# Loading x and the experts' matrices of a soft mixture of experts in rows of 2 KB

## The chip, the core and the metric

The kernel runs on one core of a Trainium2 chip. The metric is the device time of one launch in microseconds (us). The kernel before took 889.4 us as the median of three runs (888.58, 889.4 and 891.3).

## What is computed

Two stages stand behind one another. The first is a long causal convolution per channel of u = x * v with a filter that a small network computes from position features; its result is multiplied by x again. The reference uses Fourier transforms, the kernel matrix products. The second is a soft mixture of experts over all 45,824 tokens of 128 features that the first stage gives:

```python
logits = x @ phi                                  # (N, 32): 8 experts, 4 slots each
d = exp(logits - logits.max(0)); d /= d.sum(0)    # over the tokens, per slot
slot_input = d.T @ x                              # (32, 128): dispatch
for e in range(8):
    slot_out[e] = maximum(slot_input[e] @ w1[e], 0) @ w2[e]   # w1: 128x1024, w2: 1024x128
c = exp(logits - logits.max(1)); c /= c.sum(1)    # over the slots, per token
out = c @ slot_out                                # (N, 128): combine
```

All data are float32.

## The kernel before

The convolution runs over eight groups of channels. Its last phase (`p4`, seven steps of the list ORDER, lines 623 to 636) multiplies by x (`p4_gate`, or `p4_gate_apart` on GpSimd) and stores the result to a scratch buffer in HBM, `scr`, features as rows and tokens as columns (`p4_out`, line 465; `p4_rest`, line 471). The tokens stand there in pieces, two for each step of ORDER: most of 3,296 tokens, one of 2,884 and two last ones of 44 and 48. A row of a piece is one contiguous run.

The second stage (`Moe` and `_moe`) reads `scr` back in 23 blocks of 2,048 tokens (NB = 16 times 128; the last has 768). A block is a tile of 128 partitions (features) by 2,048 tokens, 1 MB, with rows of 8 KB. `Moe.load` (line 692) issues one DMA for each piece that a block touches, so one or two a block (line 700). Where the buffers are:

- blocks 0 to 4 go to `ahead_buf`, in the place where the experts' matrices will be. Their first 112 rows (d0 = 0 to D - CG) are loaded while the convolution's last group is still on its way (`weights`, line 655), the last 16 rows (d0 = 112) in `ahead` (line 722) when these have been stored. Blocks 5 to 9 (`xbuf`) follow in `ahead` too, between the stores of the last steps.
- the loop of `_moe` works on pairs of blocks. Blocks i and up are transposed (`turn`, line 714), and `fetch(i)` (line 952) then issues what comes into the buffer that is free now: for i below 10 the block i + 10, for 10 to 13 two experts' `w1` each (`load_w1`, line 670, 512 KB with rows of 4 KB), for 14 the `w2` of experts 0 to 2 (`load_w2`, line 673, the same size), for 15 to 17 the blocks 20 to 22, then the other `w2`.
- step m of the loop has, on TensorE in this order: the transposes of block 2m, the logits (line 780) of blocks 2m + 2 and 2m + 3, the transposes of block 2m + 1, the dispatch sums of pair m - 1 (line 872) and the running maximum (line 820). The last pair but one that is whole, blocks 20 and 21, has its logits in step 9.

After the last block the dispatch sums become the slots' inputs, the experts run (lines 1067 to 1106), and the combine step (`spread`, line 1120) makes one output tile after another (line 1128) and stores it in 1 MB DMAs (line 1136).

Every load and store of this part is issued by SyncE, one behind the other. Instructions inside `inorder(...)` keep the program's order; the loads of x and of the matrices are not in it, and their place is a scheduler's. A DMA is issued when the buffer that it overwrites has been read, when what it reads has landed, and when the semaphore that it will use is free of its last transfer.

Of the kernel before, what the change touches and what calls it, by code (L numbers as in the profile page):

```python
# [17 lines left out]
B, S, D = 4, 11456, 128  # L18
# [27 lines left out]
FF = 1024  # L46
# [592 lines left out]
class Moe:  # L639
# [3 lines left out]
    XB = 5  # L643
    OB = 4
    CB = 8 * NB

    def __init__(self, tc, cp, scr, phi, mw1, mw2, rep, out):
        self.tc, self.cp, self.scr, self.out = tc, cp, scr, out
        self.phi, self.mw1, self.mw2, self.rep = phi, mw1, mw2, rep

        self.blocks = [(q, min(self.NB, QN - q)) for q in range(0, QN, self.NB)]
        self.xt, self.xq = {}, {}
        self.pieces = sorted(_pieces().values())
# [14 lines left out]
            self.load(i, 0, D - CG)  # L668

    def load_w1(self, e):  # L670
        self.tc.nc.sync.dma_start(out=self.w1t[:, e], in_=self.mw1[e])

    def load_w2(self, e):
        self.tc.nc.sync.dma_start(out=self.w2t[e],
                                  in_=self.mw2[e])

    def logit_banks(self):
        self.pls = self.ctx.enter_context(ExitStack())
# [3 lines left out]
    def places(self):  # L682
# [4 lines left out]
        bufs = [self.xreg[:, i * sz : (i + 1) * sz] for i in range(n)]  # L687
        far = [self.E[:, self.CB * NSLOT + i * sz :][:, :sz] for i in range(2)]
        self.xbuf = bufs[: self.XB - 1] + far[:1]
        self.obuf = bufs[self.XB - 1 :] + far[1:]  # L690

    def load(self, i, d0=0, d1=D):
        q0, n = self.blocks[i]
        t = (self.ahead_buf if i // self.XB in (0, 2) else self.xbuf)[i % self.XB][:, : 128 * n]
        z0, z1 = 128 * q0, 128 * (q0 + n)
        for a, m in self.pieces:
            lo, hi = max(z0, a), min(z1, a + B * m)
            if lo < hi:
                src = self.scr[D * a : D * (a + B * m)].rearrange("(d t) -> d t", d=D)
                self.tc.nc.sync.dma_start(out=t[d0:d1, lo - z0 : hi - z0], in_=src[d0:d1, lo - a : hi - a])  # L700
        self.xt[i] = t.rearrange("p (q t) -> p q t", t=128)

    def turn(self, pool, tag, i, k0, k1, shared=False):
# [28 lines left out]
def _moe(mo):  # L732
# [11 lines left out]
    ereg = mo.E  # L744
    far = mo.CB * NSLOT + 4 * FF
    Cms = [ereg[:, : mo.CB * NSLOT], ereg[:, far : far + (QN - mo.CB) * NSLOT]]
    Cms = [c.rearrange("p (q s) -> p q s", s=NSLOT) for c in Cms]
    csum = ereg[:, QN * NSLOT + 4 * FF :][:, :QN]

    def weights_of(q0, n):  # L750
        assert (q0 < mo.CB) == (q0 + n <= mo.CB)
        return Cms[0][:, q0 : q0 + n] if q0 < mo.CB else Cms[1][:, q0 - mo.CB : q0 - mo.CB + n]

# [198 lines left out]
    def fetch(i):  # L952
        if i < 2 * XB:
            mo.load(i + 2 * XB)
        elif i < 2 * XB + 4:
            for e in range(2 * (i - 2 * XB), 2 * (i - 2 * XB) + 2):
                mo.load_w1(e)
        elif i < 3 * XB:
            for e in range(3):
                mo.load_w2(e)  # L960
        elif i + XB < NBL:
            mo.load(i + XB)
        else:
            for e in range(3 + 2 * (i + XB - NBL), min(NEXP, 5 + 2 * (i + XB - NBL))):
                load_w2(e, i)
# [330 lines left out]
```

## Time and profile before

| | |
|---|---|
| median of three runs | 889.4 us |
| profiled execution | 892.43 us |
| its span, from the first to the last instruction | 890.7 us |
| TensorE busy with matmuls | 857.9 us (96%) |
| VectorE, ScalarE, GpSimd busy | 80%, 51%, 44% |
| DMA over the span | 197.02 MB, 221 GB/s on the mean, 94,386 packets |
| granted TensorE clock, mean | 0.992 |

A busy share is a mean over unlike stages. A DMA share of 1.0 means that all 16 DMA engines are occupied by packets; it says nothing of how fast these are, for which the rate in GB/s stands beside it. "Issue" in the chain of waits is time in which an engine waited for nothing that the profile shows.

### The profile page before, as it was taken

The numbers are of one execution on the slowest core, as the hardware profiler recorded it, in microseconds if no ns is written. First come the engines' busy times: TensorE is split into PE (matmuls) and PEld (weight loads), VectorE is DVE, ScalarE is ACT, GpSimd is POOL, SyncE is SP. The second block draws the span as 40 slices with busy tenths as digits, with TensorE's granted clock in tenths as the row PEclk, the third lists the DMA queues.
The fourth block names the chain that finished last, engine by engine and source line by source line (L and its number), as shares of the span: only waits on it lengthen the run. The fifth ranks groups of instructions, "written<-read, shape, count | busy, mean of one in ns | idle before, by whom it ended". The sixth has DMA issues, their size and how long they took to land. (4 is left out here: it accounts for less than half of the span.)

```text
span 890.7 us, 37282 instructions
## 1 busy us (share of the span) xinstructions
PE 857.9 (96%) x16192; PEld 791.0 (89%) x16192; DVE 714.5 (80%) x1239; ACT 455.1 (51%) x971; POOL 393.1 (44%) x538
## 2 busy tenths in 40 slices
PE   9999999999999999999999999999999999899991
PEld 8998989999999999999999999999999987566540
DVE  5967976799799889988988998899789058786791
ACT  5775558315811851472166128415811637887761
POOL 5003860492088019405910960393078013775750
PEclk9999999999999999999999999999999999999996
DMA  9963684457747754775486376557716979993698
GB/s 323 396 197 117 204 246 153 144 155 254 207 135 207 234 166 128 237 237 172 132 261 202 120 222 214 168 166 247 218 44 173 272 176 374 412 355 121 277 416 365
DMA packets 94386, 197.02 MB, mean 221 GB/s; under 512 B 14329, under 2 KB 55707, under 8 KB 90382
## 3 DMA queue, kind: packets, MB, share of 16 engines
q1 hardware_dynamic: 94046, 194.50, 67.0%
q8 instruction: 128, 2.10, 0.9%
q14 instruction: 36, 0.29, 0.1%
q10 hardware_dynamic: 144, 0.07, 0.0%
q0 software_dynamic: 32, 0.07, 0.0%
HBM read 137.73 MB, written 56.86 MB: 218 GB/s over the span
## 5 line engine op out<-in xcount | busy, mean ns | idle before, releaser
L350 POOL TENSOR_TENSOR T<-m 111x256 f32<-111x256 f32 (+1 forms) x199 | 150.9, 758 | 344.8 <-DVE m L344 344.8
L344 DVE TENSOR_TENSOR m<-p,T 111x1024 f32<-111x1024 f32 (+1 forms) x175 | 200.4, 1205 | 14.4 <-PE p L340 7.6
L360 PE MATMUL p<-tab,T 111*99 111x112 f32 x2048 | 205.4, 260 | 1.4 <-POOL T L351 0.3
L360 PEld LDWEIGHTS p<-tab,T 111*99 111x99 f32 x2048 | 198.8, 170 | 6.5 <-issue 1.6
L340 PE MATMUL p<-T,W 128*64 128x128 f32 (+1 forms) x3168 | 197.3, 276 | 0.4 <-issue 0.3
L425 ACT ACTIVATE vc<-p 128x412 f32<-128x412 f32 (+1 forms) x112 | 51.7, 513 | 266.4 <-PE p L412 227.0
L340 PEld LDWEIGHTS p<-T,W 128*64 128x64 f32 (+1 forms) x3168 | 182.0, 127 | 2.8 <-DVE m L344 0.6
L412 PE MATMUL p<-tab,E 99*64 99x103 f32 (+1 forms) x3584 | 174.0, 252 | 1.6 <-DVE E L373 0.6
L412 PEld LDWEIGHTS p<-tab,E 99*64 99x64 f32 x3584 | 166.2, 136 | 3.8 <-ACT vc L425 0.8
L375 ACT ACTIVATE E<-p 99x448 f32<-99x448 f32 x254 | 131.9, 575 | 63.9 <-PE p L360 57.8
L351 POOL TENSOR_TENSOR T<-m 111x256 f32<-111x256 f32 (+1 forms) x199 | 147.4, 741 | 0.0
L186 ACT ACTIVATE T<-p 128x396 f32<-128x396 f32 x240 | 100.2, 535 | 11.3 <-PE p L174 11.1
L174 PE MATMUL p<-tab1x,x 53*64 53x99 f32 x3648 | 86.7, 246 | 0.2 <-ACT E L224 0.2
L174 PEld LDWEIGHTS p<-tab1x,x 53*64 53x64 f32 x3648 | 79.8, 132 | 4.4 <-ACT E L224 0.4
L443 DVE TENSOR_TENSOR p<-p,vc 128x824 f32<-128x824 f32 (+1 forms) x46 | 47.0, 1022 | 8.9 <-ACT vc L425 8.9
L268 DVE TENSOR_TENSOR x<-x,T 128x448 f32<-128x448 f32 x51 | 31.6, 619 | 21.2 <-DMA x<-in_xf_dram 11.6
L274 DVE TENSOR_TENSOR x<-T 128x224 f32<-128x224 f32 x102 | 39.2, 426 | 1.8
L270 DVE TENSOR_TENSOR T<-x 128x224 f32<-128x224 f32 x102 | 39.2, 426 | 1.7
L224 ACT ACTIVATE E<-fl 111x512 f32<-111x512 f32 (+1 forms) x50 | 26.8, 627 | 21.3 <-PE fl L218 21.3
L451 DVE TENSOR_TENSOR E<-p,E 128x824 f32<-128x824 f32 x36 | 36.6, 1017 | 1.2
L720 ACT ACTIVATE xreg<-pt 128x512 f32<-128x512 f32 (+1 forms) x68 | 35.0, 609 | 1.0 <-PE pt L714 0.9
L344 DVE TENSOR_TENSOR m<-p,E 111x1024 f32<-111x1024 f32 (+1 forms) x25 | 28.7, 1201 | 5.1 <-PE p L340 4.9
(156 smaller groups left out, 972.1 us busy)
## 6 DMA issues: line engine op xcount, KB each, us to landing
x<-in_xf_dram SPq DMA_DIRECT2D x114, 256.0 KB, 4.2
out_dram<-xreg SPq DMA_DIRECT2D x16, 1024.0 KB, 10.6
E<-in_xi_dram SPq DMA_DIRECT2D x37, 412.0 KB, 3.9
T<-in_vf_dram SPq DMA_DIRECT2D x65, 224.0 KB, 5.1
scr<-E SPq DMA_DIRECT2D x67, 206.0 KB, 4.3
T<-hs SPq DMA_DIRECT2D x63, 154.0 KB, 4.5
hs<-E SPq DMA_DIRECT2D x12, 784.0 KB, 4.6
mv<-in_vf_dram SPq DMA_DIRECT2D x42, 224.0 KB, 4.6
```

The costliest lines, as they stand in the source:

```text
L174: inorder(nc.tensor.matmul(ps[h][RP * d : RP * d + RP, i, s, :], lhsT=sd[js, i, s, d, :], rhs=tab1x[js, J * (s + d) : J * (s + d + 1)], st ...
L186: inorder(nc.scalar.activation(dst, src, AF.Copy))
L270: inorder(eng.tensor_tensor(out=vt[:, :, m : m + 2], in0=xr[:, :, 0:2], in1=xr[:, :, 2:4], op=op))
L340: inorder(nc.tensor.matmul(ps[ns, i].rearrange("p b c -> p (b c)"), lhsT=W[:, k0 + i, ns], rhs=Tf[:, :, k0 + i, :], start=True, stop=True, ...
L344: inorder(nc.vector.tensor_mul(m[:, :n].rearrange("p k s e c i -> p k s (e c i)").rearrange("p k s (b c) -> p k s b c", c=CG), ps[:, :n].u ...
L350: inorder(eng.tensor_tensor(out=Ty[:, 0], in0=m[:, :n, 0, 0], in1=m[:, :n, 1, 1], op=ALU.subtract))
L351: inorder(eng.tensor_tensor(out=Ty[:, 1], in0=m[:, :n, 1, 0], in1=m[:, :n, 0, 1], op=ALU.add))
L360: inorder(nc.tensor.matmul(pk[:, i, 2 * s : 2 * s + 2, :].rearrange("p q r -> p (q r)"), lhsT=T[0:N1, s, 2 * k + i, u // 2, :, u % 2], rhs ...
L375: inorder(nc.scalar.activation(dst, src, AF.Copy))
L412: inorder(nc.tensor.matmul(pv[RP * h : RP * h + RP, 2 * k + i, w, j0:], lhsT=E[:J, r, 2 - 2 * w + s, :], rhs=tab4[:, s, o + j0 : o + NJ], ...
L425: inorder(nc.scalar.activation(vc[:, w, :, j0:], pv[:, :, 0, j0:], AF.Copy, scale=2.0 * w - 1.0))
L443: inorder(nc.vector.tensor_tensor(out=pw[:, :, :, j0:], in1=vc[:, :, :, j0:], op=ALU.add, in0=pw[:, 1:2, :, j0:].to_broadcast([128, 2, 4, ...
```

## The change

`Moe` gets a constant RUN = 512. `load` cuts what it reads of a piece at every 512 tokens of the block, where the first row is 0 (`d0 == 0`), so that a transfer has rows of 2 KB at most; with d0 = 112, the last 16 rows of blocks 0 to 4, it stays as it was. `load_w1` and `load_w2` load an expert's matrix in two halves with rows of 2 KB.

```diff
+    RUN = 512
 
     def load_w1(self, e):
-        self.tc.nc.sync.dma_start(out=self.w1t[:, e], in_=self.mw1[e])
+        for f in range(0, FF, self.RUN):
+            self.tc.nc.sync.dma_start(out=self.w1t[:, e, f : f + self.RUN], in_=self.mw1[e, :, f : f + self.RUN])
 
     def load_w2(self, e):
-        self.tc.nc.sync.dma_start(out=self.w2t[e],
-                                  in_=self.mw2[e])
+        n = self.RUN // 128
+        for j in range(0, FF // 128, n):
+            self.tc.nc.sync.dma_start(out=self.w2t[e][:, j : j + n], in_=self.mw2[e, :, j : j + n])
 
         for a, m in self.pieces:
-            lo, hi = max(z0, a), min(z1, a + B * m)
-            if lo < hi:
-                src = self.scr[D * a : D * (a + B * m)].rearrange("(d t) -> d t", d=D)
+            lo, end = max(z0, a), min(z1, a + B * m)
+            src = self.scr[D * a : D * (a + B * m)].rearrange("(d t) -> d t", d=D)
+            while lo < end:
+                hi = min(end, z0 + ((lo - z0) // self.RUN + 1) * self.RUN) if d0 == 0 else end
                 self.tc.nc.sync.dma_start(out=t[d0:d1, lo - z0 : hi - z0], in_=src[d0:d1, lo - a : hi - a])
+                lo = hi
```

## Rows read from the trace of the kernel before

**Rows 1.** Windows: stretch, length, busy us by engine, clock, DMA share, GB/s.

```profile
840.00:860.00 20.00, 19.28 (x116) 8.50 (x112) 18.87 (x34) 14.75 (x27) 18.20 (x29) 1.00 1.01 417
```

**Rows 2.** Chain of waits, 640 us to the end: start, length, what.

```profile
771.66 0.95 issue
...
778.60 0.70 issue
...
784.97 1.03 issue
...
801.80 1.92 PE pl L780 x16
...
814.13 0.62 issue
...
828.99 3.07 PE pw L1128 x23
```

**Rows 3.** The page, DMA queues: packets, MB, share of 16 engines.

```profile
q8 instruction: 128, 2.10, 0.9%
```

**Rows 4.** TensorE's waits, 757 to 829: total us, times, longest.

```profile
PE pt L714 <- issue: 1.6, 2, 1.0
```

**Rows 5.** Windows again, columns as in the first group.

```profile
12.00:15.00 3.00, 3.00 (x30) 3.00 (x29) 2.08 (x4) 1.19 (x2) 0.40 (x2) 1.00 1.05 354
15.00:18.00 3.00, 3.00 (x29) 2.85 (x28) 2.54 (x5) 1.64 (x5) 0.00 (x0) 1.00 1.05 382
18.00:21.00 3.00, 2.83 (x24) 2.46 (x26) 2.94 (x11) 0.85 (x3) 0.00 (x0) 1.00 1.05 387
...
757.00:775.00 18.00, 15.67 (x322) 9.90 (x317) 14.47 (x25) 16.90 (x37) 13.54 (x14) 1.00 1.02 415
775.00:790.00 15.00, 13.27 (x298) 9.22 (x294) 11.23 (x23) 11.94 (x27) 11.09 (x14) 1.00 1.02 406
790.00:800.00 10.00, 10.00 (x242) 7.60 (x242) 9.11 (x19) 9.38 (x21) 9.61 (x11) 1.00 0.95 345
```

**Rows 6.** DMA issues in 791.2 to 791.9: size, us from issue to landing.

```profile
xreg<-scr SPq DMA_DIRECT2D x1, 738.0 KB, 7.2
xreg<-scr SPq DMA_DIRECT2D x1, 286.0 KB, 7.5
```

**Rows 7.** DMA issues in 794.8 to 795.1.

```profile
xreg<-scr SPq DMA_DIRECT2D x1, 1024.0 KB, 6.7
```

**Rows 8.** DMA issues in 752.5 to 753.1.

```profile
ffw<-scr SPq DMA_DIRECT2D x1, 752.0 KB, 9.6
```

**Rows 9.** Timeline of TensorE, 764 to 768: start, length, instructions.

```profile
764.47 1.06 PE L780 MATMUL pl<-ffw,aux 128*32 128x512 f32 x8
```

**Rows 10.** Timeline of SyncE's queue, 680 to 800.

```profile
698.16 4.17 SPq L700 DMA_DIRECT2D ffw<-scr  x6
...
720.96 1.74 SPq L465 DMA_DIRECT2D scr<-xl  x2
...
729.10 2.58 SPq L700 DMA_DIRECT2D ffw<-scr  x5
731.79 0.36 SPq L700 DMA_DIRECT2D xreg<-scr  x1
...
737.37 2.53 SPq L465 DMA_DIRECT2D scr<-E  x2
...
751.40 6.79 SPq L700 DMA_DIRECT2D ffw<-scr  x8
```

**Rows 11.** SyncE's waits, 690 to 752: total us, times, longest.

```profile
SPq L465 <- DVE aux L726: 14.7, 1, 14.7
SPq L465 <- DMA xreg<-scr: 3.6, 3, 1.6
```

**Rows 12.** DMA traffic from 15 to 21 us.

```profile
DMA packets 1313, 2.31 MB, mean 384 GB/s; under 512 B 147, under 2 KB 750, under 8 KB 1312
...
E<-in_xf_dram SPq DMA_DIRECT2D x3, 256.0 KB, 6.0
```

## Prediction, made before the changed kernel had run

> **What bounds the kernel now.** I read four views, from the end backwards. The windows give the stage that sets the end: from 840 us the DMA engines are busy throughout and write the output at 417 GB/s [rows 1]. The first output tile is ready right after the combine step's first matmuls at 828.99 [rows 2], so whatever moves that moment moves the end with it, one to one. The chain of waits from 757 to 829 is almost only TensorE, block after block of tokens: transposes (L714), logits (L780), dispatch sums (L872). It holds four stops of TensorE put down to "issue", 0.95, 0.70, 1.03 and 0.62 us [rows 2], the first three inside a run of equal matmuls, 6 to 7 us apart. A stop that no semaphore explains, and that returns at equal distances while the engine runs through its code at an even pace, looks like waiting for the next piece of code, and the page has a queue that fetches code in packets of 16 KB [rows 3]. The list of TensorE's waits in this stretch has "issue" on top [rows 4] and no DMA anywhere in it: no load of x is late today.
>
> The third view is the DMA traffic of the same stretch. The engines' share is 1.02 with 415 and 406 GB/s from 757 to 790 and 0.95 with 345 from 790 to 800 [rows 5]. Data move in the order of issue, so a load that is issued in this time waits behind all before it. The last two full blocks show how little room is left. Block 20 is issued at 791.2 in two parts that land 7.2 and 7.5 us later [rows 6], at about 799.1; block 21 goes out at 794.85 and lands 6.7 us later [rows 7], at 801.6. Their logits start at 801.80 and take 1.92 us for both [rows 2], so block 21 is read from 802.7: it is there 1.1 us early. An early block has more: the second part of block 11, issued at 752.5, lands 9.6 us later at 762.1 [rows 8], while the logits of blocks 10 and 11 begin at 764.47 [rows 9].
>
> The fourth view is SyncE's queue. Five split-off loads take 2.58 us, 0.52 us each [rows 10]. And it holds at most eight transfers in flight: of the two stores that follow at 737.37, the second is the ninth issue after the single load at 731.79 (2, 1 and 3 issues lie between), it stretches the pair to 2.53 us [rows 10], and waits of this kind are put down to the landing of such a load, 3.6 us for three of them [rows 11].
>
> **The change, part by part.** *Counts.* A block of 2048 tokens is 1 MB and now goes in one or two transfers. Split at every 512 tokens and at the pieces' borders it takes four or five. Counted over the 23 blocks the x loads go from 46 to 113 (the eight 16-row slices stay whole, as d0 is not 0 there) and the experts' matrices from 16 to 32. No byte more is moved.
>
> *Rate of the transfers, the term that decides.* Before, rows of x are mostly 8 KB and go at 415 and 406 GB/s; I use 411. The trace has the new shape too: from 15 to 21 us the queue carries transfers of 256 KB, 128 rows of 2 KB, and some with rows a little shorter, and the mean is 384 GB/s [rows 12], 382 and 387 in the two halves with a share of 1.05 [rows 5]: as busy as engines get. Between the landings of block 5 and block 21, blocks 6 to 21 (16 MB) and the weights w1 and the first two of w2 (5 MB) pass, 22.0 million bytes: 53.5 us at 411, 57.3 us at 384, so 3.8 us more. Bounds: nothing at 411; 8.6 us at 354, the lowest window of that early stretch [rows 5]. I take 384, since its transfers are nearest in size.
>
> *What absorbs it.* Block 21 has 1.1 us in hand. From 790 to 800 the share is 0.95 [rows 5]; a fuller queue would use those 0.5 us. So TensorE comes to wait for block 21 by 3.8 - 1.1 - 0.5 = 2.2 us, and everything behind it moves by as much. Block 11, with some 3 us in hand, meets only the delay of six blocks, 6.3 million bytes, 1.1 us, and stays hidden.
>
> *TensorE's stops.* If code comes sooner between smaller packets, up to 0.95 + 0.70 + 1.03 = 2.7 us go away before 790. They are worth nothing on the main path: TensorE then arrives at block 20 earlier and waits longer for the same landing. Only the stop at 814.13, behind the last wait, can come off the end: 0 to 0.62, of which I count 0.4, as the matrices that pass just ahead of it have half the row length.
>
> The page "DMA: Bandwidth & Descriptors" of the Trainium skill says, in Queues, rings and completion order, that an engine finishes a whole packet of one queue before it turns to the next. That fits shorter waits of code behind shorter rows, and no row here measures that wait by itself. By it the first three stops would go, which leaves the sum where it is.
>
> *SyncE's time.* From block 10's load at 751.40 [rows 10] to the landing of block 21, 75 issues by 0.52 us are 39 of 50 us: hidden, as long as the transfers (17.8 million bytes in 75, 0.62 us each at 384) are slower than the issues. Before that, from 729.10 to 751.40, 24 issues become 39, 20.3 of 22.3 us: just hidden, with 0 to 2 us to lose; I take 0. What is queued there behind the loads are the last stores to scratch and the last gate's x load, which GpSimd waits for, beside the path. Earlier still, the five blocks that are fetched ahead (eight issues, six of them in 4.17 us from 698.16 [rows 10]) grow by 15 issues or 7.8 us, and SyncE afterwards stood idle for 14.7 us until VectorE let the next store go [rows 11]: nothing lost, and 2 us if the 112-row parts land slower.
>
> *TensorE's waits.* A block's logits now wait for up to five landings. These waits ride on matmuls that run back to back in the trace; nothing, at most 0.05 us a block on 12 pairs, 0.6 us.
>
> *Sum.* 2.2 - 0.4 = +1.8 us. The profiled execution took 892.43 us (span 890.7, 1.7 around it), 3.0 above the median of the three runs, 889.4; I put the difference on the median: 891.2 us. Low end of the same case: 395 GB/s (22.0 million bytes in 55.7, +2.2), all of the reserves and of the stop: 2.2 - 1.1 - 0.5 - 0.62 = 0. High end: 3.8 with no reserve but the 1.1, 0.6 for waits and 1 for SyncE, +4.3.
>
> The same page, in Rules for kernel authors, asks for 1 MiB a DMA and more, which speaks against this change. Its fit of 2.0 us and bytes by 436 GB/s for one DMA would make an estimate of 10.4 us for four quarters against 4.4 for the whole if they ran one by one. They do not: 384 GB/s with quarters stands in the rows, and the rule enters only as a milder loss.
>
> **Rivals.** *A gain from code.* The stops go and short rows cost nothing. Then block 21's landing bounds: 1.1 + 0.5 + 0.62 = 2.2 us saved, 887.2; with the queue also drained sooner the whole 3.3, 886.1. For it: the stops are real and on the chain. Against it: 384 against 411, and a share at 1.0, which leaves no earlier landing. 0.17, of which 0.10 above 2.7 us. *Eight short transfers do not keep the engines full.* Eight are now 2 MB in flight where up to 8 MB stood; where small border pieces (16 to 48 KB) fill the slots, the queue runs thin and the rate falls to the 354 of the early window: 8.6 - 1.1 - 0.5 = +7.0, 896.4. It decides, as slower by over 0.3%, from about 380 GB/s down. For it: the early window itself. Against it: the two windows behind that one. 0.22. *SyncE is late at 720.* If the fetched-ahead parts hold it beyond the reserve, the stores at 720.96 [rows 10] and the last rows of blocks 0 and 1 slip, and the first logits with them: +2 to 3 us on top, 893.5. 0.05. *The change does nothing that counts*, because each landing keeps its reserve: 889.4. 0.08.
>
> **How the numbers follow.** A difference below 0.3% (2.7 us) can't be told from none here. The forecast has 0.48; about a quarter of it lies above 2.7 us. Faster: 0.10. Slower: 0.12 + 0.22 + 0.04 = 0.38. Same: the remaining 0.52. The range leaves out the full gain, about one in ten below 886.6, and the worst of thin queues, about one in ten above 896.0.
>
> **What would show it.** Right: the rate from 757 to 790 falls to 380 to 395 with the share still at 1.0; the landings after issue drop to some 5 us while blocks land later; TensorE's list gains a wait before the logits of blocks 20 and 21; the stops at 772, 779 and 785 shrink; the first output matmul comes near 831. Wrong: the rate holds at 410 and no wait appears before those logits, or the share falls below 0.95 in the middle of the stretch (the thin queue), or TensorE's wait shows up before the first logits at 732.

## The result, and the profile after

The changed kernel takes 900.2 us, the median of six runs (899.45 to 903.39), beside 889.9 for the kernel before; the ratio is 1.0124, with an interval of 1.0103 to 1.0145. Forecast were 891.2 and at most 896.0. The profiled execution took 902.52 us with a span of 900.7, 10.0 us longer than the span before.

The chain of waits of the changed kernel, 795 to 845 us (start, length, what), shows where they lie. pl L785 are the logits, pw L1133 the first output matmuls:

```profile
798.02 6.35 DMA ffw<-in_mw_dram
804.43 4.70 DMA xreg<-scr
809.27 1.97 PE pl L785 x8
811.96 1.94 PE pl L785 x8
...
838.99 3.07 PE pw L1133 x23
```

The first output matmul stands at 838.99 instead of 828.99 [rows 2], and the span is longer by the same 10.0 us. TensorE's waits of the changed kernel from 700 to 845 (total us, times, longest) hold one long one:

```profile
PE pl L785 <- DMA xreg<-scr: 10.1, 1, 10.1
PE pl L785 <- DMA ffw<-scr: 0.8, 1, 0.8
PE pl L785 <- DVE rm L808: 0.8, 1, 0.8
```

No line put down to "issue" is left in that list, where [rows 4] had one on top: the stops are gone. Without them TensorE is done with the work ahead of block 20 at 799.15, 2.65 us earlier than the 801.80 of [rows 2], and then stands for 10.1 us until block 20 is there.

SyncE's queue of the changed kernel shows why block 20 is late (start, length, line, count):

```profile
787.69 9.98 SPq L673 DMA_DIRECT2D ffw<-in_mw_dram  x16
798.02 2.78 SPq L678 DMA_DIRECT2D ffw<-in_mw_dram  x4
801.72 7.96 SPq L704 DMA_DIRECT2D xreg<-scr  x13
```

Block 20 is issued at 801.72, 10.5 us after the 791.2 of [rows 6], behind the 5 MB of w1 and w2. Everything ahead of it was late too, and the windows of the changed kernel say why (stretch, length, busy us of PE, PEld, DVE, ACT and POOL, clock, DMA share, GB/s):

```profile
757.00:775.00 18.00, 16.69 (x347) 10.85 (x343) 14.57 (x26) 16.69 (x37) 13.64 (x14) 1.00 0.98 327
775.00:790.00 15.00, 14.74 (x343) 10.69 (x345) 13.46 (x27) 14.35 (x31) 13.12 (x16) 1.00 1.00 341
790.00:800.00 10.00, 9.15 (x220) 6.80 (x208) 9.11 (x20) 8.79 (x22) 7.72 (x10) 1.00 0.98 339
800.00:805.00 5.00, 0.00 (x0) 0.00 (x0) 1.26 (x2) 1.71 (x4) 3.77 (x3) 0.78 1.05 386
805.00:810.00 5.00, 0.73 (x4) 0.23 (x8) 0.00 (x0) 0.00 (x0) 0.00 (x0) 0.50 1.03 369
810.00:815.00 5.00, 4.24 (x38) 1.41 (x32) 2.55 (x6) 0.02 (x1) 0.00 (x0) 0.50 0.87 287
815.00:820.00 5.00, 5.00 (x130) 4.42 (x130) 2.15 (x6) 3.62 (x10) 0.00 (x0) 0.86 0.70 225
```

The reader sees two things. The loads run at 327 to 341 GB/s where [rows 5] had 415 and 406, and the DMA engines' share is 0.98 to 1.00 all the same: by the share alone nobody would say that anything is missing. And after TensorE has stood still, its granted clock is 0.50 from 805 to 815, which is 1.2 instead of 2.4 GHz: the logits of blocks 20 and 21, 1.92 us for both in [rows 2], take 1.97 and 1.94 in the chain above.

By the chain the 10.0 us are: 2.65 gained by the stops, 10.12 lost in the wait (together +7.47, 801.80 to 809.27), and +2.53 behind it (29.72 instead of 27.19 us from the first of these logits to the first output matmul). Of the last, 1.97 + 1.94 - 1.92 = 2.0 are the logits at half the clock and 0.8 the wait between them, less the stop of 0.62 that is gone; 0.4 is left for the other matmuls at the low clock.

The list puts the 0.8 down to VectorE's maximum (rm), and there the landing times in the trace say otherwise. Block 20's last transfer lands at 809.13 and its logits begin at 809.27; block 21's last transfer lands at 811.83 and its logits begin at 811.96, as close behind it. So TensorE waits for a load a second time, and block 20's logits, slow as they are, end before block 21 is there and cost nothing. What moves the end is block 21: its logits begin 9.2 us later than before (811.96 instead of 802.76), take 1.0 longer at half the clock, the stop gives 0.6 back, and 0.4 is left for the matmuls behind.

### The profile page after: what moved, and what is told of

The parts are those of the page before. It is cut to its first block, busy times and chain, and to the rows that moved or that the text cites. A ratio compares the mean times of both kernels' runs of the same rounds, so it can differ in the third digit from the quotient of the medians.

```text
span 900.7 us, 37458 instructions
## 1 busy us (share of the span) xinstructions
PE 860.5 (96%) x16192; PEld 793.4 (88%) x16192; DVE 714.6 (79%) x1239; ACT 455.1 (51%) x971; POOL 393.1 (44%) x538
## 5 line engine op out<-in xcount | busy, mean ns | idle before, releaser
L344 DVE TENSOR_TENSOR m<-p,T 111x1024 f32<-111x1024 f32 (+1 forms) x175 | 200.4, 1205 | 12.6 <-POOL T L351 6.0
```

The source lines that it names most:

```text
L344: inorder(nc.vector.tensor_mul(m[:, :n].rearrange("p k s e c i -> p k s (e c i)").rearrange("p k s (b c) -> p k s b c", c=CG), ps[:, :n].u ...
```

## The experiments

Theory A: eight transfers can be in flight, and at 256 KB each they are too few bytes to keep the rate up. Theory C: the rate falls because the rows are 2 KB long. "Rate" below is that from 760 to 790 us of one profile, where these kernels load x and the matrices: 410 GB/s before, 333 in the changed kernel. "MB" is what was under way in the same stretch, the mean over time of the bytes of all SyncE transfers between issue and landing. "Wait" is TensorE's wait ahead of the logits of blocks 20 and 21, as far as the profile puts it down to a DMA. Ratios are to the kernel before, beside it on the same chip.

| kernel | x: KB at most, rows | rate | MB | share | wait, us | median, us | ratio (interval) |
|---|---|---|---|---|---|---|---|
| before | 1024, 8 KB | 410 | 4.2 | 1.02 | none | 889.9 | 1 |
| the change | 256, 2 KB | 333 | 1.6 | 0.99 | 10.1 | 900.2 | 1.0124 (1.0103 to 1.0145) |
| x_only | 256, 2 KB | 359 | 1.8 | 1.02 | 7.3 | 898.6 | 1.0080 (1.0051 to 1.0109) |
| w_only | 1024, 8 KB | 393 | 3.7 | 1.01 | none | 890.4 | 0.9997 (0.9981 to 1.0012) |
| run1024 | 512, 4 KB | 403 | 3.3 | 1.03 | 0.5 | 890.7 | 0.9990 (0.9977 to 1.0003) |
| rows2k_big | 512, 0.2 to 2 KB | 363 | 2.6 | 1.05 | 6.0 | 898.6 | 1.0081 (1.0054 to 1.0108) |
| rows2k_pair | 512, 2 KB | 377 | 2.5 | 1.04 | see text | 896.6 | 1.0059 (1.0040 to 1.0078) |
| rows8k_small | 256, 8 KB | 240 | 0.8 | 0.79 | see text | 928.5 | 1.0417 (1.0382 to 1.0451) |
| rows4k_half | 256, 4 KB | 255 | 1.3 | 1.03 | 13.8 | 920.7 | 1.0339 (1.0310 to 1.0369) |
| thin2048 | 1024, 8 KB, places taken | 323 | 1.8 | 0.93 | 12.2 | 902.8 | 1.0134 (1.0102 to 1.0165) |
| thin1024 | 512, 4 KB, places taken | 347 | 1.7 | 0.97 | 10.2 | 901.9 | 1.0119 (1.0097 to 1.0141) |
| thin512 | 256, 2 KB, places taken | 261 | 0.9 | 0.88 | 18.8 | 920.1 | 1.0320 (1.0301 to 1.0339) |

**Which part.** x_only is the kernel before with the change's cut of x alone:

```diff
             while lo < end:
                 hi = min(end, z0 + ((lo - z0) // self.RUN + 1) * self.RUN) if d0 == 0 else end
                 self.tc.nc.sync.dma_start(out=t[d0:d1, lo - z0 : hi - z0], in_=src[d0:d1, lo - a : hi - a])
                 lo = hi
```

> Only the loads of x are cut at 512 tokens; the experts' matrices go whole, as before. Theory A (x in 256 KB pieces leaves too little in flight under eight semaphores, so the engines run dry while blocks 10 to 19 pass): in the changed kernel these nine landings take 29.5 us instead of 22.7 and the weights only 0.7 us more, so nearly all of the loss stays: 898 to 900 us, and TensorE waits 8 to 10 us for blocks 20 and 21. Theory B (the weights ahead of block 20 are what delays it): 890 to 893 us.

It takes 898.6 us, as A expected; the long wait of its TensorE, 700 to 845, is shorter than the 8 to 10 us expected:

```profile
PE pl L783 <- DMA xreg<-scr: 7.3, 1, 7.3
```

w_only has the other half, the matrices alone:

```diff
-        self.tc.nc.sync.dma_start(out=self.w1t[:, e], in_=self.mw1[e])
+        for f in range(0, FF, self.RUN):
+            self.tc.nc.sync.dma_start(out=self.w1t[:, e, f : f + self.RUN], in_=self.mw1[e, :, f : f + self.RUN])
```

> Only the experts' matrices go in halves; x is loaded as before. Theory A: 0.7 us more in the passing of the weights, less than the 1.1 us that block 21 had in hand: 889 to 890.5 us. Theory B: most of the 10 us, 896 to 900.

890.4 us and no wait for DMA: a story that blames the halved matrices by themselves falls. Whether they cost something on top of the cut of x isn't clear: the ratios are 1.0124 and 1.0080, and their intervals just overlap.

run1024 is the change with RUN = 1024: x in at most 512 KB with rows of 4 KB, the matrices whole (FF is 1024).

```diff
-    RUN = 512
+    RUN = 1024
```

> RUN is 1024 instead of 512: x in transfers of up to 512 KB with rows of 4 KB, the matrices whole as before. If the loss comes from how few bytes eight transfers hold (theory A), twice the bytes keep the engines full: rate from 760 to 780 at 395 to 412 GB/s, a wait of at most 2 us for blocks 20 and 21, 887 to 891 us. If any cut of x costs by its count of transfers or by SyncE's time, about half of the loss stays: 893 to 896.

890.7 us, not to be told from before. Its windows and, for its x loads from 757 to 790, size and us to landing:

```profile
760.00:790.00 30.00, 27.65 (x599) 19.36 (x599) 23.86 (x46) 26.43 (x57) 21.87 (x28) 1.00 1.03 403
```

```profile
xreg<-scr SPq DMA_DIRECT2D x7, 512.0 KB, 7.8
ffw<-scr SPq DMA_DIRECT2D x3, 512.0 KB, 7.7
```

403 GB/s by 7.8 us is 3.1 MB under way, near the 3.3 of the table. The same view of the changed kernel:

```profile
ffw<-scr SPq DMA_DIRECT2D x15, 256.0 KB, 4.7
xreg<-scr SPq DMA_DIRECT2D x14, 256.0 KB, 6.1
```

333 by 4.7 to 6.1 is 1.6 to 2.0 MB, where the table has 1.6. The number of transfers under way is the same as before, 7.0 on the mean in both kernels; each is smaller. The step from half to a quarter of the old size costs everything, the step from whole to half nothing. Both theories allow that: size and row were halved together.

**Attempts to part size and row.** rows2k_big keeps large transfers and makes the rows short: each load goes as two, of every other run of columns.

```diff
+                o, s = (v.rearrange("p (x y r) -> p y x r", x=2, y=2) for v in (o, s))
+                for y in range(2):
+                    self.tc.nc.sync.dma_start(out=o[:, y], in_=s[:, y])
```

> Each load of x is issued as two transfers that interleave (chunks 0 and 2, chunks 1 and 3 of its run), so that rows are 2 KB at most as in the change, but a transfer is up to 512 KB; the matrices whole. Theory A: twice the bytes in flight, engines full, only the price of short rows is left (384 against 411 GB/s): about 2 to 3 us over before, 891 to 893, a wait of 1 to 3 us for blocks 20 and 21. Theory C (short rows themselves are slow in this stretch): 898 to 900 as with the change, rate 760 to 780 near 340 GB/s.

898.6 us, what C expected, at 352 GB/s from 760 to 780 where C expected about 340, and with 2.6 MB under way, more than x_only. But its rows go down to 192 bytes, shorter than the change's, so the point for C isn't clean. rows2k_pair mends that: the change's own cuts, with the first and third and the second and fourth run of a piece going out as one transfer of up to 512 KB with rows of 2 KB.

```diff
+                n, far = hi - lo, (lo + 2 * self.RUN, hi + 2 * self.RUN)
+                if n == self.RUN and far in parts:
+                    parts.remove(far)
+                    o, s = t[d0:d1, lo - z0 : far[1] - z0], src[d0:d1, lo - a :][:, : 3 * n]
+                    o, s = (v.rearrange("p (j r) -> p j r", r=n)[:, 0:3:2] for v in (o, s))
```

> Cut exactly as in the change, but two full chunks that are not neighbours (0 and 2, 1 and 3 of a block within one piece) go in one transfer, so the rows are the change's, a transfer is up to 512 KB, and fewer are issued; the matrices whole. It is the clean form of the first test with paired chunks, whose rows were 0.6 to 2 KB. Theory A: less of the loss than with x cut alone (898.6), 892 to 895. Theory C (row length is what counts): 898 to 899 again.

896.6 us, between the two. Its windows:

```profile
760.00:790.00 30.00, 27.83 (x605) 19.41 (x601) 24.23 (x47) 26.79 (x59) 22.53 (x27) 1.00 1.04 377
```

The rows are those of x_only, the matrices are whole in both, and 18 GB/s come back (359 to 377) with the bytes in flight: its full loads land after 6.3 us, 377 by 6.3 is 2.4 MB. It still lacks 26 of run1024's 403. The 18 alone would not show much: order512, below, has the change's own transfers in this stretch, 1.6 MB under way, and a rate of 363, so profiles of equal transfers differ by up to 30. TensorE waits here too, 1.67 and 1.65 us ahead of the two blocks' logits. The profile puts that down to ScalarE and VectorE, but the blocks' last transfers land at 802.38 and 805.09 and the logits begin at 802.52 and 805.23.

The opposite test, long rows in small transfers, failed twice. rows8k_small sends each x load as four transfers of every fourth row:

```diff
+                o, s = (v.rearrange("(p j) t -> j p t", j=n) for v in (o, s))
+                for j in range(n):
+                    self.tc.nc.sync.dma_start(out=o[j], in_=s[j])
```

> Each whole load of x (128 rows) goes as four transfers of every fourth row: rows of 8 KB as before, at most 256 KB a transfer as in the change; the matrices whole, the 112-row parts whole. Theory A: as little in flight as in the change, so the loss stays, 896 to 902, rate 760 to 780 at 320 to 360 GB/s with blocks 20 and 21 late. Theory C: rows are long, so the time of before, 888 to 891.

Both theories missed by 26 us and more: 928.5. TensorE's list has 33.1 us put down to VectorE's rd; VectorE waits for GpSimd there, and GpSimd 17.6 and 19.4 us for a load of x. The rate is 240. The instructions of the load's line on SyncE (757 to 790; shortest, median and longest in ns, first and last start) and its queue show another cost, the issue:

```profile
L705 SPq DMA_DIRECT2D ffw<-scr x32: 538/592/1317, 762.1 to 783.0; - x32
```

```profile
762.14 21.40 SPq L705 DMA_DIRECT2D ffw<-scr  x32
```

In the changed kernel the same line reads

```profile
L704 SPq DMA_DIRECT2D ffw<-scr x21: 319/370/912, 757.0 to 770.4; - x21
```

An issue of such a transfer takes 592 ns instead of 370. The 32 carry five blocks, 5.2 MB, in 21.4 us, which is the 245 GB/s that SyncE can send, and the share of 0.79 says that the engines ran dry. rows4k_half cuts run1024's transfers at partition 64 instead:

```diff
+                for p0, p1 in (((d0, 64), (64, d1)) if d0 == 0 else ((d0, d1),)):
+                    self.tc.nc.sync.dma_start(out=t[p0:p1, lo - z0 : hi - z0], in_=src[p0:p1, lo - a : hi - a])
```

> x cut at 1024 tokens as in run1024, and each of these transfers in two, of rows 0 to 63 and of the rest: 256 KB at most with rows of 4 KB, as many transfers as in the change, weights whole. Theory A (bytes in flight: eight transfers of 256 KB are 2 MB at most): the rate between 760 and 790 is 330 to 365, a wait of 5 us or more ahead of the logits of blocks 20 and 21, 896 to 900. Theory C (the rows' length alone sets the rate): 400 to 410 GB/s as in run1024, no wait over 1 us, 889 to 892. Both together: in between.

920.7 us, again far beyond both. Here the engines are full:

```profile
760.00:790.00 30.00, 24.18 (x442) 15.83 (x446) 16.75 (x32) 18.85 (x41) 14.47 (x19) 0.83 1.03 255
```

At a share of 1.03 they move 255 GB/s: with transfers on half of the partitions a packet of 4 KB takes 262 ns (median, 760 to 790) where run1024's takes 161. That is a third cost, and says nothing for A or C.

**The test that decides.** thin2048 leaves x and the matrices as before and takes the places instead. Behind each late load (block 6 on) go transfers of one 4-byte word from one spare place in memory to another, so many that every 512 tokens, or 256 KB of a matrix, hold one of the eight places. So, as in the change, at most some 2 MB can be in flight, with rows of up to 8 KB; 1.8 are under way.

```diff
+    def also(self, n):
+        for _ in range(n):
+            k = self.extra % 128
+            self.put(out=self.spare[k : k + 1], in_=self.phi[k : k + 1, :1])
+            self.extra += 1
...
+                if i > self.XB and d1 == D:
+                    self.also(max(0, (hi - lo + 256) // 512 - 1))
```

> The kernel before (x and weights whole, rows of 8 KB at most) with transfers of one 4-byte word put between its late loads, one for each 512 tokens or 256 KB more than the first that a transfer carries, in held order, from block 6 on. They take places among the eight transfers that can be in flight, so that about 2 MB of loads are in flight, as in the change, but with long rows. Theory A (what counts is the bytes in flight): the rate between 760 and 790 falls from 410 to 330 to 365 GB/s, the logits of blocks 20 and 21 wait 4 us or more, 895 to 900. Theory C (what counts is the rows' length): 400 to 412 GB/s, no wait over 1 us, 889.5 to 893.

902.8 us, and the rate falls to 323 with no row cut:

```profile
760.00:790.00 30.00, 28.64 (x642) 19.89 (x630) 24.84 (x47) 27.56 (x61) 23.78 (x29) 1.00 0.93 323
```

thin1024 does the same to run1024 (one word behind each full transfer).

> run1024 (rows of 4 KB, 512 KB a transfer) with the same one-word transfers, one behind each of its full transfers: again about 2 MB in flight. Theory A: 330 to 365 GB/s between 760 and 790 where run1024 has 401 to 406, a wait of 4 us or more, 895 to 900. Theory C: 395 to 406 GB/s, no wait over 1.5 us, 890 to 893.

901.9 us; its windows, where run1024 has 403:

```profile
760.00:790.00 30.00, 29.74 (x679) 21.67 (x677) 25.88 (x51) 28.77 (x63) 24.93 (x30) 1.00 0.97 347
```

thin512 takes places from the change itself (one word behind every second transfer; 1.3 MB in flight were meant, 0.9 are).

> The change with a one-word transfer behind every second of its short ones: some 1.3 MB in flight instead of 2. Theory A: the rate falls further, to 230 to 300 GB/s between 760 and 790, and the time is 905 to 920. Theory C: the rate stays at 325 to 345 and the time at 898 to 902.

920.1 us, and the rate is 261. By their numbers all three go A's way: the rates lie in A's intervals or, for thin2048, 7 GB/s below, and the times at or up to 3 us beyond the upper ends of A's; C is off by 8.9 us or more in each.

A word costs SyncE time as well as a place, so its waits have to be looked at (755 to 798). In thin2048 it waits mostly for landings, which are what frees a place:

```profile
SPq L673 <- DMA ffw<-scr: 5.5, 4, 2.1
SPq L673 <- DMA xreg<-scr: 4.3, 3, 2.3
```

Of the 33 us from 757 to 790 SyncE spends 20 issuing in thin2048, 23 in thin1024 and 21 in the change, so its time doesn't set these apart. In thin512 it spends 28, waits for landings 0.4 us in all, and five of the eight places are taken on the mean:

```profile
771.59 0.58 SPq L675 DMA_DIRECT2D spare<-in_phi_dram  x1
772.27 0.83 SPq L675 DMA_DIRECT2D ffw<-scr  x2
773.16 0.56 SPq L675 DMA_DIRECT2D spare<-in_phi_dram  x1
```

So thin512 is held by SyncE, as rows8k_small is, and proves nothing about places. The other two decide: with 1.6 to 1.8 MB under way, rows of 8, 4 and 2 KB give 323, 347 and 333 to 363 GB/s, and short rows are not the slow ones. (That the words by themselves slow the loads isn't excluded by a run of its own.)

What the rows alone cost can be estimated from the packets of 760 to 790: the median one takes 312 ns for 8 KB before, 161 for 4 KB in run1024 and 84 for 2 KB in the changed kernel, so 16 engines would move 420, 407 and 390 GB/s. By this estimate the rows cost some 20 to 30 of the 77 GB/s that are lost; between rows2k_pair and run1024 stand 26, with 2.5 against 3.3 MB under way.

**Is block 20's place all of it?** order512 moves w1 and the first three w2 behind blocks 20 to 22 in the program; order2048 does so in the kernel before.

```diff
-        elif i < 2 * XB + 4:
-            for e in range(2 * (i - 2 * XB), 2 * (i - 2 * XB) + 2):
-                mo.load_w1(e)
...
+            if i + XB == NBL - 1:
+                for e in range(NEXP):
+                    mo.load_w1(e)
+                for e in range(3):
+                    mo.load_w2(e)
```

> The change as it is, with one thing moved: the experts' matrices (w1, and w2 of experts 0 to 2) are fetched behind blocks 20 to 22 instead of ahead of them. If the 10 us that TensorE waits are the late landing of blocks 20 and 21 behind the 5 MB of matrices and nothing else, they go: x still passes at 320 to 340 GB/s, no wait for those blocks, and the stops for code are gone too, 885 to 888 us. If the loss sits elsewhere (SyncE, the clock, the matmuls' waits), 896 to 900.

> The same move in the kernel before, whole transfers. There nothing waited for these loads, so the move alone should give nothing: 888 to 891 us, the stops put down to issue still there (about 3 us in all). If it gives 885 to 887, the move itself is worth the gain and the short rows nothing.

Neither told what it was made for: 899.96 (ratio 1.0091, 1.0069 to 1.0113) and 890.66 us (0.9993, 0.9979 to 1.0007). The planner put the matrices ahead of block 20 all the same, as order512's SyncE queue shows:

```profile
784.48 11.05 SPq L673 DMA_DIRECT2D ffw<-in_mw_dram  x16
795.87 2.30 SPq L678 DMA_DIRECT2D ffw<-in_mw_dram  x4
798.51 9.31 SPq L704 DMA_DIRECT2D xreg<-scr  x13
```

place512 holds the order of the late loads (keep_in_program_order on each) and spreads the matrices around the blocks:

```diff
+        elif i < 2 * XB + 3:
+            mo.load_w1(i - 2 * XB)
...
             mo.load(i + XB)
+            late = {3 * XB: (3, 5), 3 * XB + 1: (5, 6)}.get(i, (6, NEXP))
+            for e in range(*late):
+                mo.load_w1(e)
```

> The change with its weights put elsewhere and the order of the late loads held: w1 of experts 0 to 2, block 20, w1 of 3 and 4, block 21, w1 of 5, block 22, w1 of 6 and 7, w2 of 0 to 2. The changed kernel sends all of w1 ahead of block 20, though that block's buffer is free at about 792. Theory A (the ten microseconds are the wait for blocks 20 and 21 and what the clock loses after it): at 330 to 340 GB/s block 20 lands by 797 to 798 and block 21 by 800 to 801, the wait ahead of their logits falls from 10.1 to at most 2 us, the granted clock stays near 1.00 behind it, no stop of TensorE comes back, and the time is 887 to 890. Rival (the low rate costs wherever the bytes lie: weights that come later stop the experts' matmuls instead): a wait of 5 us or more at a matmul that reads ffw or xreg between 805 and 830, and 894 to 899.

896.0 us (1.0052, 1.0031 to 1.0073): 6 us beyond A's upper end, and in the interval of the rival, which also expected a wait of 5 us or more. Block 20 is in time, block 21, behind w1 of experts 3 and 4, isn't:

```profile
798.16 1.06 PE L791 MATMUL pl<-xreg,aux 128*32 128x512 f32 x8 [0.27 <-DMA xreg<-scr]
804.41 1.93 PE L791 MATMUL pl<-xreg,aux 128*32 128x512 f32 x8 [5.19 <-DMA xreg<-scr]
```

place512b sends w1 of experts 3 and 4 behind block 21 as well ((3, 3) and (3, 6) in the line above).

> place512 with w1 of experts 3 and 4 behind block 21 instead of ahead of it (w1 of 0 to 2, block 20, block 21, w1 of 3 to 5, block 22, the rest). Block 21's buffer is free at about 796 and its four transfers then have nothing ahead of them but block 20: landing by 801, the wait for it falls from 5.2 to 2 us or less, and the time to 888.5 to 892. If the rate of short rows keeps even this late (landing after 803), 893 to 896, as place512.

892.0 us (1.0017, 0.9997 to 1.0038), not to be told from before and at the upper end of what was expected, at a rate of 343. Its waits are two short ones ahead of the logits of blocks 21 and 22, 1.92 (put down to VectorE, but block 21's last transfer lands at 803.57, later than the 801 expected) and 1.24 us:

```profile
803.71 1.07 PE L791 MATMUL pl<-xreg,aux 128*32 128x512 f32 x8 [1.92 <-DVE rd L816]
810.49 0.66 PE L791 MATMUL pl<-xreg,aux 128*32 128x192 f32 x6 [1.24 <-DMA xreg<-scr]
```

So the low rate is still there (340 to 349 GB/s from 760 to 775, where place2048, below, has 412 to 415 in the same order), and nearly all of its price is gone once nothing stands ahead of the two blocks that TensorE needs next. The same order with larger transfers brings nothing:

> The same order of loads with x cut at 1024 tokens and the weights whole (512 KB a transfer at most, rows of 4 KB). Theory A: no wait for blocks 20 and 21; what is left of the stops of TensorE decides: 887 to 890. If rows of 4 KB keep the stops of the kernel before (2 to 3 us), 889 to 891.

> The same order of loads with x and the weights cut as in the kernel before: the control for the other two. In the kernel before blocks 20 and 21 are not late, so the order has nothing to give: 888.5 to 891 (within 0.2% of before), with the stops of TensorE of 0.7 to 1.0 us still there. Rival (the order alone brings what place512 brings): as place512.

892.1 us (1.0003, 0.9989 to 1.0018) and 892.2 (1.0020, 1.0007 to 1.0034): with no wait to remove they keep TensorE's stops. None of these versions beats the kernel before: short transfers without the wait win 2 to 3 us of stops and lose them in two small waits.

## Why the prediction was wrong, by its own steps

*Right: the lever and the place.* The rate fell, and the loads came late. The end moved with the first output matmul, 10.0 and 10.0 us, and the wait came ahead of the logits of blocks 20 and 21.

*Wrong: the rate, the term that was to decide.* I took 384 GB/s from the early stretch, "since its transfers are nearest in size". They were, but not in what turned out to count. Their landing took 6.0 us [rows 12], and 384 by 6.0 is 2.3 MB under way (2.1 counted as in the table); with the change 1.6 are, since pieces of blocks as small as 16 KB hold places too. rows2k_pair at 2.5 MB has 377, which is the 384 nearly. So 384 was about what rows of 2 KB cost, and the forecast put the loss from too few bytes under way at nothing. With 333 in place of 384 my own sum gives 22.0 MB in 66.1 us, 12.6 more than the 53.5; less the 0.5 of the fuller queue block 21 would land 12.1 late. It landed 10.2 late: the last of its four transfers is issued by 807.45 and they take

```profile
xreg<-scr SPq DMA_DIRECT2D x4, 256.0 KB, 4.7
```

(the changed kernel's issues from 805 to 807.4), so at about 811.8 instead of 801.6. The formula held within 2 us; its one input was bad, and its worst bound, 354, was too mild by 21 GB/s.

*Half right: the rival.* "Eight short transfers do not keep the engines full" is what happened, by its number of 2 MB, and I gave it 0.22 and 896.4 us. Its price failed with the same 354. And I gave it the wrong mark, a share below 0.95 in the middle of the stretch. The share was 0.98 to 1.00 while thin1024, where places were taken, has 0.97 at 347. A thin queue shows in the time of a packet at least as much as in idle engines: by the share, 16 engines and the rate, 4 KB took 16 x 1.03 x 4096 / 403 = 168 ns in run1024 and 16 x 0.97 x 4096 / 347 = 183 in thin1024. It is a few packets that do it: the median packet of 4 KB takes 161 and 159 ns, but 0.4% of them take more than one and a half times that in run1024 and 5.3% in thin1024, 511 ns each on the mean.

*Right in effect, open in cause: the stops.* All four are gone, and the three before block 20 were worth nothing, since TensorE only waits longer. The page "DMA: Bandwidth & Descriptors" of the Trainium skill says in Queues, rings and completion order that an engine finishes a packet before it turns to another queue. The traces don't show that it is the rows' length: run1024 with rows of 4 KB has two stops of 1.0 and 1.1 us, but thin1024 with the same rows has none, and order512 with the change's rows of 2 KB has one of 0.9. That the stops are waits for code is not shown either. The rule of the same page that I set aside as too harsh, 1 MiB a DMA and more (Rules for kernel authors), had the right sign; the trace differs in its size, since 512 KB cost nothing in run1024. (The page gives the fit that I quoted beside it for DMAs issued by GpSimd; these are SyncE's.)

*Missing: the clock.* The sum ended with the wait. After 10 us of standing still the clock was at 0.50, and that moved the end by some 1.4 us: 1.0 on block 21's logits and 0.4 on the matmuls behind. I had no row of a wait that long in the kernel before.

*Right: the small terms.* SyncE's 17 ahead-loads take 13.04 us instead of 4.17 for six and the stores follow at 721.14, 0.2 later than in [rows 10]:

```profile
698.83 13.04 SPq L704 DMA_DIRECT2D ffw<-scr  x17
...
721.14 1.92 SPq L465 DMA_DIRECT2D scr<-xl  x2
```

So the rival of a late SyncE falls. The blocks' own waits cost nothing that can be seen, and the 0.8 us for ffw in the list stands at the logits of block 11; those of block 10 start at 764.66 instead of 764.47 [rows 9].

## What to carry to other kernels

Where the number of transfers in flight is fixed, cutting them cuts the bytes under way: multiply the rate by the time from issue to landing, and compare that product, not the size of one transfer, with a stretch whose rate you want to borrow. Don't take a DMA share of 1.0 as proof that the queue is deep enough. If a stream has a microsecond of reserve, look first at what stands ahead of the next needed load: moving 3.5 of 5 MB behind the two blocks that came next gave back nearly all that the lower rate had cost. And when the profile puts a wait down to another engine, look up when the last load landed: several waits here were loads.

## What was not expected of the hardware

A wait of 10 us took TensorE's granted clock from 1.00 to 0.50, and it was still 0.50 from 810 to 815, when the engine worked again. Transfers of every fourth row took SyncE 592 ns each (median) where those of the change took 370, and transfers on 64 of the 128 partitions ran at 255 GB/s with the engines full. With few bytes under way most packets are as fast as ever and a few are slow: in the changed kernel the median of 2 KB is 84 ns, and 4% of them take 335 on the mean. Open is why they are slow: from 800 to 805, when TensorE stands still, the change's transfers of 256 KB reach 386 GB/s with 1.9 MB under way, and thin2048 and thin1024 show less of that (355 and 342 from 800 to 810, after 323 and 347). No run took that apart.
